# Turning the first unit's 47-point result on chip instead of through DRAM, and taking the token matrix's sums to GpSimd

## The chip, the cores and the metric

The kernel runs on one core of one Trainium2 chip. A core has five engines that each work through a queue of their own, in order: TensorE (PE in the profile; matrix products, with PEld for its weight loads), VectorE (DVE), ScalarE (ACT), GpSimd (POOL) and SyncE (SP, which here only issues DMAs). They meet at semaphores. SBUF is the on-chip memory that all of them read, PSUM is where the products land; DRAM is reached by DMA. The metric is the device time of one execution in microseconds (us), smaller is better. The kernel before takes 2456.34 us, the median of three runs (2453.95 to 2456.38).

## The reference

The input x is 8 batches of 3008 tokens with 256 channels. A Fourier stage comes first, then a token and channel mixer on its result:

```
X  = rfft(x, axis=1)                                # over 3008 tokens
Yr = Xr @ w_r - Xi @ w_i + b_r ;  Yi = Xr @ w_i + Xi @ w_r + b_i
Yr, Yi = soft_threshold(Yr, 0.01), soft_threshold(Yi, 0.01)
y  = irfft(Yr + 1j*Yi, n=3008, axis=1)              # batch, 3008, 256
h  = relu(y^T @ w_tok1) @ w_tok2                    # w_tok1 3008 x 256, w_tok2 256 x 3008
u  = y + h^T
out = u + relu(u @ w_ch1) @ w_ch2                   # 256 x 1536, 1536 x 256
```

x, w_r, w_i, b_r and b_i are float32; the four mixer weights (here `wt1`, `wt2`, `moe_w_ch1`, `moe_w_ch2`) are float64.

## The kernel before, in words

**The transform.** 3008 is 47 times 64, so the Fourier transform is a 47-point transform followed by a 64-point one. The 47-point part works on sums and differences of mirrored rows. Its rows are read in 13 groups of 5 x 24 = 120 rows (`NG = 13`, `GS = 5`, `KH = 24`), each with two halves `x[:, 0]` and `x[:, 1]`; the sum feeds a cosine matrix, the difference a sine matrix (`f1`, 120 x 120 blocks). `dft47` (L258) drives the 13 groups: `load`, then `sum_diff` (L220), then `stage1` (L233), which does the products, copies PSUM to SBUF and stores the result to a DRAM tensor. It is read back with the 64 x 2 rows of one pair of frequencies on the partitions, because the 64-point transform (`forward`, L414) takes its products over these. There are 12 such pairs, `kp` = 0 to 11.

**The units.** The 8 batches are treated as units `[0], [1], [2,3], [4,5], [6,7]`. Unit 0 is computed in `begin` (L547) with plain float32 products; the later units use pairs of rounded products (`mm3`, L174) and are woven into the channel mixer of the unit before them.

**What `begin` does.** It does two things side by side. One is unit 0: `forward` (line L421 does its products, L423 the copy from PSUM, L424 the third plane `xf` as a sum of the other two), `mix` (L441 the products with w_r and w_i, L446 to L448 the reads of PSUM with the bias on DVE, L450 to L452 the soft threshold, whose result stays in the tiles `held`), `inverse` (L469) and `tokens` (L484). The other is the token matrix w_tok1: its 13 groups are loaded as float64 (`raw`), made float32 by `narrow` (L144 to L156: two ACT instructions and six DVE instructions a group), passed through the same 47-point products as x, stored to the DRAM tensor `a_w`, read back (`load_w`) and taken through the 64-point transform in `make_w` (L317). Since the transform of y against the token matrix is taken in the frequency domain, `tokens` needs both.

For the token matrix the kernel before forms no sums. It puts both halves into the products (L250 to L252):

```
PE.matmul(pt[:120, o:o + w], lhsT=f1[:, i], rhs=sd[:, 0], start=True, stop=False)
PE.matmul(pt[:120, o:o + w], lhsT=f1[:, 2 * i], rhs=sd[:, 1], start=False, stop=True)
```

which is four products a group, where a sum and a difference would need two.

**The loop over steps.** After unit 0's 47-point part, `begin` runs steps n = 0 to 18. Step n takes the next two groups of the token matrix (until the 13 are done), `forward(n)`, `mix(n-1)`, `inverse(n-3)`, and from step 7 on `tokens` and `make_w`. Three groups of the token matrix are done ahead of step 0, so the groups end in step 4. The loads of unit 0's result from DRAM (`load_a`, L411) run three steps ahead. The float64 pieces of w_ch1 are narrowed and split in steps 8 to 13, those of w_ch2 and the first of w_tok2 after that. Then `channel` begins, the mixer over 49 chunks of at most 512 columns. It runs to the end of the kernel, with the later units' transforms woven in.

**What sets the order.** The order on each engine is a list that is fixed when the program is built; a scheduling layer makes it from the program's order and the tiles' buffers, so it is not exactly the source's order. Each engine takes its list in order and waits at the head for what the head needs. All products share four PSUM banks in rotation (`bank`, L129): a bank is written again only after ACT or DVE has read it. All loads, and unit 0's and the token matrix's stores, are on SP's queue, in order.

## Time and profile before

| what | value |
|---|---|
| runs | 2453.95, 2456.34, 2456.38 us |
| the profiled execution's own time | 2458.71 us |
| its span | 2456.7 us |
| PE busy | 2423.6 us (99%) |
| DVE, ACT, POOL busy | 1107.5 (45%), 873.3 (36%), 305.1 (12%) us |
| HBM read and written | 162.68 and 87.43 MB |

The profile's rows give a start and a length in us, the engine, the line of the code, the operation, the tile written and the tiles read, their sizes and how many instructions are merged. A float32 product appears as two records. In brackets stands the engine's idle time ahead of the row and what ended it. A matmul's recorded length contains some 0.16 us of pipeline, so the pace of TensorE is read from start to start. Rows of the "stretches" view give, for a stretch of time, the length, each engine's busy time with the number of records, the clock granted to TensorE (1.00 is full), the busy share of the DMA engines and GB/s.

### The profile page before, as it was taken

Reading aid. Unit: us, or ns where it says so; the run is one execution under the profiler, and the core shown is the slowest. Engines: PE = TensorE matmul, PEld = TensorE weight load, DVE = VectorE, ACT = ScalarE, POOL = GpSimd, SP = SyncE. Lnnn points to the kernel's source line nnn. Section 1 sums busy time; section 2 is a strip of 40 time slices with the busy share of each in tenths; the row PEclk is TensorE's granted clock in tenths of the full one; section 3 lists DMA queues with packets and bytes.
Section 4 is the critical chain, followed back from the end, with each engine's and each line's share of the span. In section 5 each row is a group of like instructions: output and inputs, shape, how many; then the busy total and the mean of one; then the engine's idle time right before and its main releaser. Section 6 shows DMA issues by size and latency. Waiting matters only on the chain.

```text
span 2456.7 us, 31566 instructions
## 1 busy us (share of the span) xinstructions
PE 2423.6 (99%) x12748; PEld 2108.6 (86%) x12748; DVE 1107.5 (45%) x1773; ACT 873.3 (36%) x1583; POOL 305.1 (12%) x259
## 2 busy tenths in 40 slices
PE   6999999999999999999999999999999999999999
PEld 5878999988888888888888898888888888888887
DVE  6975665454544444434344354434334333232332
ACT  4764444443334343333333343333333222222222
POOL 0000222222222111111111111111111000000000
PEclk8999999999999999999999999999999999999999
DMA  9775334552233462222222263222321112112110
GB/s 269 238 244 152 95 112 141 156 174 90 84 98 111 114 179 84 65 72 88 89 76 69 94 176 105 80 87 80 101 66 38 63 56 63 49 58 80 37 55 18
DMA packets 148946, 252.15 MB, mean 103 GB/s; under 512 B 11009, under 2 KB 101089, under 8 KB 148801
## 3 DMA queue, kind: packets, MB, share of 16 engines
q1 hardware_dynamic: 122289, 199.80, 27.2%
q10 hardware_dynamic: 26512, 50.34, 6.5%
q8 instruction: 100, 1.64, 0.3%
q14 instruction: 45, 0.37, 0.0%
HBM read 162.68 MB, written 87.43 MB: 102 GB/s over the span
## 4 chain that ended last, share of the span: by engine, by line
PE 93%; DMA 4%; DVE 1%; ACT 1%; SPq 0%; issue 0%; POOL 0%; DVEq 0%; ACTq 0%
PE ph L175 10%; PE ph L176 10%; PE po L175 10%; PE po L177 10%; PE po L176 10%; PE ph L177 10%; PE pu L708 4%; PE px L421 3%; PE pm L177 2%; PE pm L175 2%; PE pm L176 2%; PE pu L175 2%; PE pu L176 2%; PE pu L177 2%; PE gp L175 2%; PE gp L177 2%
## 5 line engine op out<-in xcount | busy, mean ns | idle before, releaser
L747 DVE SCALAR_TENSOR_TENSOR hlo<-ph,hh 128x512 fp32r<-128x512 f32 (+4 forms) x588 | 391.6, 667 | 646.0 <-ACT hh L746 643.0
L746 ACT ACTIVATE hh<-ph 128x512 fp32r<-128x512 f32 (+4 forms) x588 | 340.5, 580 | 815.8 <-PE ph L177 812.9
L175 PE MATMUL ph<-uh,w 128*128 128x512 f32 (+4 forms) x1176 | 456.0, 388 | 0.4 <-DVE hlo L747 0.3
L176 PE MATMUL ph<-ul,w 128*128 128x512 f32 (+4 forms) x1176 | 449.6, 382 | 0.3 <-DVE ul L717 0.3
L177 PE MATMUL ph<-uh,w 128*128 128x512 f32 (+4 forms) x1176 | 448.8, 382 | 0.0
L175 PE MATMUL po<-hh,w2h 128*128 128x512 f32 (+4 forms) x1176 | 448.7, 382 | 0.0
L176 PE MATMUL po<-hlo,w2h 128*128 128x512 f32 (+4 forms) x1176 | 448.1, 381 | 0.0
L177 PE MATMUL po<-hh,w2l 128*128 128x512 f32 (+4 forms) x1176 | 448.0, 381 | 0.0
L177 PEld LDWEIGHTS ph<-uh,w 128*128 128x128 f32 x1176 | 221.1, 188 | 39.4
L175 PEld LDWEIGHTS po<-hh,w2h 128*128 128x128 f32 x1176 | 221.1, 188 | 38.7
L176 PEld LDWEIGHTS po<-hlo,w2h 128*128 128x128 f32 x1176 | 221.0, 188 | 38.7 <-DVE hlo L747 0.2
L177 PEld LDWEIGHTS po<-hh,w2l 128*128 128x128 f32 x1176 | 220.9, 188 | 38.4
L175 PEld LDWEIGHTS ph<-uh,w 128*128 128x128 f32 x1176 | 221.5, 188 | 35.8 <-DVE hlo L747 1.4
L176 PEld LDWEIGHTS ph<-ul,w 128*128 128x128 f32 x1176 | 221.6, 188 | 34.6 <-DVE ul L717 0.7
L137 DVE TENSOR_TENSOR xtl<-xf,xth 128x768 fp32r<-128x768 f32 x84 | 80.5, 958 | 193.7 <-ACT xth L134 193.5
L715 ACT COPY uf<-pu 128x470 f32<-128x470 f32 (+23 forms) x188 | 62.6, 375 | 233.0 <-PE pu L708 233.0
L175 PE MATMUL pm<-wmh,xth 128*128 128x256 f32 x504 | 144.5, 287 | 0.1
L137 POOL TENSOR_TENSOR yl<-z,yh 128x512 fp32r<-128x512 f32 x72 | 92.7, 1288 | 413.2 <-ACT yh L134 413.2
L177 PE MATMUL pm<-wmh,xtl 128*128 128x256 f32 x504 | 142.5, 283 | 0.4 <-DVE xtl L137 0.3
L176 PE MATMUL pm<-wml,xth 128*128 128x256 f32 x504 | 142.4, 283 | 0.0
L708 PEld LDWEIGHTS pu<-g,b 96*128 96x128 f32 x1024 | 130.8, 191 | 3.4
L424 POOL TENSOR_TENSOR xf<-xf 128x256 f32<-128x256 f32 x84 | 69.7, 830 | 499.8 <-ACT xf L423 499.4
(124 smaller groups left out, 3213.5 us busy)
## 6 DMA issues: line engine op xcount, KB each, us to landing
wt<-wt_d SPq DMA_DIRECT2D x28, 940.0 KB, 5.5
x<-in_x SPq DMA_DIRECT2D x39, 480.0 KB, 4.3
a<-a_d SPq DMA_DIRECT2D x36, 512.0 KB, 3.9
b_d<-bt ACTq DMA_DIRECT2D x36, 512.0 KB, 3.3
out<-o SPq DMA_DIRECT2D x34, 512.0 KB, 2.8
a_d<-a ACTq DMA_DIRECT2D x36, 480.0 KB, 3.3
wt<-wt_d SPq DMA_DIRECT2D x21, 752.0 KB, 5.1
b<-b_d SPq DMA_DIRECT2D x32, 480.0 KB, 6.2
```

The source lines that it names most:

```text
L137: lo_eng.tensor_tensor(out=lo, in0=src, in1=hi.bitcast(F32), op=ALU.subtract)
L175: PE.matmul(out, lhsT=wh, rhs=xh, start=start, stop=False)
L176: PE.matmul(out, lhsT=wh, rhs=xl, start=False, stop=False)
L177: PE.matmul(out, lhsT=wl, rhs=xh, start=False, stop=stop)
L421: PE.matmul(pt[:, o:o + 128], lhsT=x, rhs=f2cols(2 * kp + ab), start=True, stop=True)
L424: (V if plain else G).tensor_tensor(out=xf[:, 0], in0=xf[:, 1], in1=xf[:, 2], op=ALU.add)
L708: PE.matmul(pt[:, s * TOKS:(s + 1) * TOKS], lhsT=b2[:, s, cs], rhs=g2[:, 0 if s0 + s == 0 else 1], start=False, stop=s == k - 1)
L715: S.copy(out=ufs[m][:, ct, lo - at:hi - at], in_=pt[:, lo - c0:hi - c0])
L746: S.activation(out=hh, in_=pt, func=AF.Relu)
L747: V.scalar_tensor_tensor(out=hlo, in0=pt, scalar=0.0, in1=hh.bitcast(F32), op0=ALU.max, op1=ALU.subtract)
```

## The change

- Unit 0's 47-point result no longer goes to DRAM. The products are turned round: the x group is the stationary operand and `f1` the moving one, so that the 256 channels come out on the partitions (two halves of 128). ACT copies each group into a tile `z` that stays in SBUF (`stage1_turned`). For each pair `kp`, `turn` takes four 128 x 128 products of `z` with the identity, which puts the 64 x 2 rows on the partitions, and ACT copies the PSUM bank to `a2`. 13 stores and 12 loads of the DRAM tensor `a_0` are gone, and four copies of one element that held back the w_r, w_i and bias loads.
- `sum_diff` always forms the sum on GpSimd. The difference is formed on the engine `eng`: on VectorE for units 0 and 1 (as before), on GpSimd for the later units (on VectorE before) and on GpSimd for the token matrix, which had no sums before and now takes two products a group.
- For unit 0, the third plane `xf` and the last subtraction of the soft threshold (`held`) go from VectorE to GpSimd.
- The order of loads and of steps: all of unit 0's x first, then the identity, `f2`, w_r, w_i, the biases and five `raw` tiles (five buffers where there were four); the token matrix's groups start in step 0, two a step, and end in step 6; they are loaded three ahead; the splits of w_ch1 come in steps 11 to 15, since `z` lies in their place until then.

```
-            raw = pool.tile([rows, n, 2], U32, name="raw", bufs=4)
+            raw = pool.tile([rows, n, 2], U32, name="raw", bufs=5)
...
-    def sum_diff(x, w, eng, pool):
-        if pool is not None and w == DT and eng is None:
-            return x
-        sd = t4([120, 2, w], "sd")
-        eng.tensor_tensor(out=sd[:, 0], in0=x[:, 0], in1=x[:, 1], op=ALU.add)
-        V.tensor_tensor(out=sd[:, 1], in0=x[:, 0], in1=x[:, 1], op=ALU.subtract)
+    def sum_diff(x, g, w, eng, pool):
+        sd = t4([120, 2, w], "sd") if pool is None else wk.tile([120, 2, w], F32, tag=("xtl", "xf", "wt", "et")[g % 4], name="sd", bufs=2)
+        G.tensor_tensor(out=sd[:, 0], in0=x[:, 0], in1=x[:, 1], op=ALU.add)
+        eng.tensor_tensor(out=sd[:, 1], in0=x[:, 0], in1=x[:, 1], op=ALU.subtract)
         return sd
...
-                elif not adds:
+                else:
                     PE.matmul(pt[:120, o:o + w], lhsT=f1[:, i], rhs=sd[:, i], start=True, stop=True)
-                else:
-                    PE.matmul(pt[:120, o:o + w], lhsT=f1[:, i], rhs=sd[:, 0], start=True, stop=False)
-                    PE.matmul(pt[:120, o:o + w], lhsT=f1[:, 2 * i], rhs=sd[:, 1], start=False, stop=True)
...
+    def stage1_turned(sd, z, g):
+        n = GS if g < NG - 1 else N2 - GS * (NG - 1)
+        pt = bank("p1")
+        for t in range(2):
+            for i in range(2):
+                o = (2 * t + i) * GS * KH
+                PE.matmul(pt[:, o:o + GS * KH], lhsT=sd[:, i, t * 128:(t + 1) * 128], rhs=f1[:, i], start=True, stop=True)
+        S.copy(
+            out=z.rearrange("p k (q n) -> p q n k", q=4)[:, :, g * GS:g * GS + n],
+            in_=pt[:, :4 * GS * KH].rearrange("p (q n k) -> p q n k", q=4, n=GS)[:, :, :n],
+        )
...
-        return dft47(load, a_w, DT, 2, None, pool)
+        return dft47(load, a_w, DT, 3, G, pool)
...
+        def turn(kp):
+            pt = bank("pz")
+            for ab in range(2):
+                for t in range(2):
+                    PE.matmul(pt[:, ab * C + t * 128:ab * C + (t + 1) * 128], lhsT=wc["z"][:, 2 * kp + ab, t * 128:(t + 1) * 128], rhs=wc["eye"], start=True, stop=True)
+            a2 = ld([128, 2, nb, C], "a2")
+            S.copy(out=a2.rearrange("p k b c -> p (k b c)"), in_=pt)
             return a2
...
-            (V if plain else G).tensor_tensor(out=xf[:, 0], in0=xf[:, 1], in1=xf[:, 2], op=ALU.add)
+            G.tensor_tensor(out=xf[:, 0], in0=xf[:, 1], in1=xf[:, 2], op=ALU.add)
...
-                V.tensor_tensor(out=yh, in0=y, in1=cl, op=ALU.subtract)
+                G.tensor_tensor(out=yh, in0=y, in1=cl, op=ALU.subtract)
...
-            x = dft47(p.load_unit, p.a, p.w, NG, V, early)
+            wc["eye"] = early.tile([128, 128], F32, name="eye")
+            z = wc["z"] = const.tile([128, KH, 2 * 128], F32, tag="w1", name="z")
+            x = dft47(p.load_unit, z, p.w, NG, V, early, True)
             next(x)
+            DMA.dma_start(out=wc["eye"], in_=io["eye"])
             DMA.dma_start(out=f2, in_=io["f2"])
+            load_mix()
+            for _ in range(5):
+                load_raw1()
...
-            a2s = {0: p.load_a(0)}
-            prepare_mix()
-            a2s[1] = p.load_a(1)
-            for _ in range(3):
-                next(w1)
-            a2s[2] = p.load_a(2)
+            a2s = {0: p.turn(0), 1: p.turn(1)}
+            next(w1)
...
-                    if n + 3 < KP:
-                        a2s[n + 3] = p.load_a(n + 3)
+                    if n + 2 < KP:
+                        a2s[n + 2] = p.turn(n + 2)
...
+                if n == KP - 1:
+                    wc["w1"] = const.tile([128, 2, 2, DF], F32R, tag="w1", name="w1")
+                if 0 <= n - KP + 1 < 5:
+                    split_w1(*pieces[n - KP + 1], wide.pop(n - KP + 1))
```

How this moves the instructions shows at three places. The first is TensorE's list at step 1: the last product or two of the token matrix's group ahead of `forward(1)` (`px`), and what follows up to `mix(0)` (`pm`). Before:

```order
L251 MATMUL p_424<-wide,f_69 120x256
L252 MATMUL p_424<-wide,f_69 120x256
L421 MATMUL px<-f_71,a_275 128x128 x4
L441 MATMUL pm_441<-wf_262,xf 128x256 x2
L441 MATMUL pm_442<-wsum,xf 128x256 x4
L251 MATMUL p_466<-wide,f_69 120x256
```

In the change the same place, with both of the step's groups (`p_382`, `p_402`) and the turn (`pz`):

```order
L242 MATMUL p_382<-sd,f_69 120x256 x2
L242 MATMUL p_402<-sd,f_69 120x256 x2
L431 MATMUL px<-f_71,a_263 128x128 x4
L419 MATMUL pz<-eye,z 128x128 x4
L451 MATMUL pm_422<-wf_114,xf 128x256 x2
L451 MATMUL pm_423<-wsum,xf 128x256 x4
```

A group has two products where it had four, they read the sums `sd` and not `wide`, and four products with the identity stand between `forward` and `mix`.

The second is VectorE's list from one `mix` (the three instructions that read `pm`) to the next narrowing of groups. Before (`held` and `xf` are unit 0's; `wide_456` and `wide_473` are two groups of the token matrix):

```order
L446 TENSOR_TENSOR z_449<-pm1_441,bias_74 128x512
L150 TENSOR_SCALAR wide_456<-wide_456 120x512
L447 TENSOR_TENSOR z_449<-pm2_442,z_449 128x256
L448 TENSOR_TENSOR z_449<-pm2_442,z_449 128x256
L151 TENSOR_SCALAR wide_456<-raw_354 120x512
L151 TENSOR_SCALAR wide_473<-raw_373 120x512
L152 SCALAR_TENSOR_TENSOR wide_456<-wide_456 120x512
L150 TENSOR_SCALAR wide_473<-wide_473 120x512
L153 TENSOR_SCALAR wide_456<-wide_456 120x512
L152 SCALAR_TENSOR_TENSOR wide_473<-wide_473 120x512
L452 TENSOR_TENSOR held_343<-z_449 128x512
```

In the change (the narrowing's lines are one higher, and `mix(0)` now stands behind seven groups):

```order
L456 TENSOR_TENSOR z_430<-pm1_422,bias_74 128x512
L156 TENSOR_TENSOR wide_387<-wide_387 120x512
L457 TENSOR_TENSOR z_430<-pm2_423,z_430 128x256
L458 TENSOR_TENSOR z_430<-pm2_423,z_430 128x256
L151 TENSOR_SCALAR wide_437<-wide_437 120x512
L152 TENSOR_SCALAR wide_437<-raw_296 120x512
L151 TENSOR_SCALAR wide_457<-wide_457 120x512
L153 SCALAR_TENSOR_TENSOR wide_437<-wide_437 120x512
L152 TENSOR_SCALAR wide_457<-raw_321 120x512
L154 TENSOR_SCALAR wide_437<-wide_437 120x512
L153 SCALAR_TENSOR_TENSOR wide_457<-wide_457 120x512
L155 TENSOR_TENSOR wide_437<-raw_296,wide_437 120x512
```

`held` and `xf` are gone from VectorE's list; the narrowing and the three reads of PSUM are what is left.

The third is GpSimd's list. Before, its first work is unit 1's (`wt`, the split of a weight block, and later `xf`, `y`):

```order
L137 ISA
L137 TENSOR_TENSOR wt_2305<-aw_2080,wt_2305 128x512
L137 TENSOR_TENSOR wt_2415<-aw_2084,wt_2415 128x512
L424 TENSOR_TENSOR xf_2095<-xf_2095 128x256
L424 TENSOR_TENSOR xf_2109<-xf_2109 128x256
L137 TENSOR_TENSOR y_2137<-z_2158,y_2137 128x512
```

In the change, one step's worth of it (`wide_367` to `wide_437` are groups 5 to 7 of the token matrix):

```order
L222 TENSOR_TENSOR sd_398<-wide_367 120x256
L223 TENSOR_TENSOR sd_398<-wide_367 120x256
L222 TENSOR_TENSOR sd_448<-wide_387 120x256
L223 TENSOR_TENSOR sd_448<-wide_387 120x256
L434 TENSOR_TENSOR xf_480<-xf_480 128x256
L462 TENSOR_TENSOR held_304<-z_430 128x512
L222 TENSOR_TENSOR sd_466<-wide_437 120x256
L223 TENSOR_TENSOR sd_466<-wide_437 120x256
```

Each step has six instructions there, on an engine that had none in `begin` but the two for `wt` at its end.

More of the change, by code (lines that the diff above doesn't have):

```diff
@@ L110, in _constants @@
         "f1": f1.astype(f),
+        "eye": np.eye(128).astype(f),
         "f2": f2.astype(f),
@@ L209, in tile_kernel @@
     a_d = [dram.tile([128, KH, 512], F32, name=f"a_d{p}") for p in range(2)]
-    a_0 = dram.tile([128, KH, C], F32, name="a_0")
     b_d = [dram.tile([NSLOT, 96, 512], F32, name=f"b_d{p}") for p in range(2)]
@@ L231, in split_x, with stage1 @@
         return xh, xl
-    def stage1(sd, dst, g, w, pool, adds):
+    def stage1(sd, dst, g, w, pool):
         n = GS if g < NG - 1 else N2 - GS * (NG - 1)
-        if pool is None:
-            a = ev([120, 2, w], "a")
-        elif adds:
-            a = pool.tile([120, 2, w], F32, name="a", bufs=4)
-        else:
-            a = wk.tile([120, 2, w], F32, tag=("xtl", "xf", "wt", "et")[g % 4], name="a", bufs=2)
+        a = ev([120, 2, w], "a") if pool is None else pool.tile([120, 2, w], F32, name="a", bufs=4)
         each = 512 // w
@@ L247, in stage1, with dft47 @@
                     mm3(pt[:120, o:o + w], f1r[:, 0, i], f1r[:, 1, i], sd[0][:, i], sd[1][:, i], True, True)
-                elif not adds:
+                else:
                     PE.matmul(pt[:120, o:o + w], lhsT=f1[:, i], rhs=sd[:, i], start=True, stop=True)
-                else:
-                    PE.matmul(pt[:120, o:o + w], lhsT=f1[:, i], rhs=sd[:, 0], start=True, stop=False)
-                    PE.matmul(pt[:120, o:o + w], lhsT=f1[:, 2 * i], rhs=sd[:, 1], start=False, stop=True)
             S.copy(out=a[:, i0:i0 + each].rearrange("p i w -> p (i w)"), in_=pt[:120])
-        wc["a"] = a
         rows = dst.rearrange("(i n) k w -> (n k) i w", i=2)
         (DMA if pool else PUT).dma_start(out=rows[g * 120:g * 120 + n * KH, :, :w], in_=a[:n * KH])
-    def dft47(load, dst, w, ahead, eng, pool=None):
+    def stage1_turned(sd, z, g):
[9 more added lines that the diff above has]
+        )
+    def dft47(load, dst, w, ahead, eng, pool=None, turned=False):
         xs = [load(g) for g in range(ahead)]
@@ L272, in dft47 @@
         prepare(0)
-        if pool is None:
-            prepare(1)
-            divide(0)
+        prepare(1)
+        divide(0)
         for g in range(NG):
@@ L278, in dft47 @@
                 xs.append(load(g + ahead))
-            prepare(g + (1 if pool else 2))
+            prepare(g + 2)
             divide(g + 1)
-            stage1(sds.pop(g), dst, g, w, pool, eng is None)
+            if turned:
+                stage1_turned(sds.pop(g), dst, g)
+            else:
+                stage1(sds.pop(g), dst, g, w, pool)
             yield 0.7 * w / C
@@ L341, in split_e, with load_mix @@
         return et
-    def prepare_mix():
-        wf = const.tile([128, 2, 2, C], F32, tag="gl", name="wf2")
-        for i in range(2):
-            V.tensor_copy(out=wf[:1, i, 0, :1], in_=wc["a"][:1, 0, :1])
-            V.tensor_copy(out=bias[:1, i, :1], in_=wc["a"][:1, 0, :1])
+    def load_mix():
+        wf = wc["wf2"] = const.tile([128, 2, 2, C], F32, tag="gl", name="wf2")
         for i, name in enumerate(("w_r", "w_i")):
@@ L387, in parts @@
         w = nb * C
-        a, bd = a_0 if plain else a_d[u % 2], b_d[u % 2]
+        a, bd = a_d[u % 2], b_d[u % 2]
         def load_unit(g):
@@ L401, in load_unit @@
             DMA.dma_start(out=x, in_=src[:, :, bs[0] % 2:bs[0] % 2 + nb])
-            if plain and g in (5, 8, 11):
-                load_raw1()
             return x.rearrange("q i b c -> q i (b c)")
@@ L560, in ahead @@
             wide[i] = narrow_w1(*pieces[i], early if i < 5 else None)
-            if i:
-                split_w1(*pieces[i - 1], wide.pop(i - 1))
         with tc.tile_pool(name="early", bufs=1) as early:
```

10 lines of the change are left out of this document (6 added, 4 removed).

## The prediction, made before the result was known

> **What bounds the kernel now.** First the page's busy times, then the stretches of time, then TensorE's rows in order of time.
>
> ```profile
> PE 2423.6 (99%) x12748; PEld 2108.6 (86%) x12748; DVE 1107.5 (45%) x1773; ACT 873.3 (36%) x1583; POOL 305.1 (12%) x259
> ```
>
> ```profile
> 0.00:29.00 29.00, 16.60 (x52) 11.64 (x53) 15.51 (x40) 12.33 (x24) 0.20 (x4) 0.90 0.88 237
> ...
> 94.00:165.00 71.00, 66.08 (x358) 50.05 (x359) 54.97 (x113) 46.41 (x98) 2.70 (x2) 1.00 0.80 247
> ...
> 240.00:2457.00 2217.00, 2209.30 (x11670) 1932.93 (x11668) 928.82 (x1400) 735.87 (x1324) 301.93 (x253) 1.00 0.30 89
> ```
>
> From 240 us on PE is idle for 7.7 of 2217 us at full clock, and the change gives PE no more and no less to do there. So only the preparation counts: the time moves by as much as the first product of `channel` moves, at 165.26.
>
> ```profile
> 27.49 2.06 PE L249 MATMUL p<-sd,f 120*120 120x256 f32 x4 [2.72 <-ACT a L253]
> 29.34 1.06 PE L251 MATMUL p<-wide,f 120*120 120x256 f32 x2
> ...
> 33.61 0.60 PE L252 MATMUL p<-wide,f 120*120 120x256 f32 x2
> ...
> 48.33 1.06 PE L421 MATMUL px<-f,a 128*128 128x128 f32 x8
> ...
> 58.09 0.60 PE L251 MATMUL p<-wide,f 120*120 120x256 f32 x2
> ...
> 61.55 1.06 PE L421 MATMUL px<-f,a 128*128 128x128 f32 x8
> ...
> 69.03 1.06 PE L421 MATMUL px<-f,a 128*128 128x128 f32 x8
> ...
> 76.88 1.06 PE L421 MATMUL px<-f,a 128*128 128x128 f32 x8
> ...
> 81.23 1.06 PE L421 MATMUL px<-f,a 128*128 128x128 f32 x8
> 82.12 1.02 PE L441 MATMUL pm<-wf,xf 128*128 128x256 f32 x4
> ...
> 84.71 1.03 PE L469 MATMUL pi<-held,ef 128*128 128x256 f32 x4
> 85.58 1.05 PE L421 MATMUL px<-f,a 128*128 128x128 f32 x8
> ...
> 91.68 1.89 PE L441 MATMUL pm<-wsum,xf 128*128 128x256 f32 x8
> ...
> 95.38 1.09 PE L317 MATMUL pw<-aw,fk 128*64 128x256 f32 x8
> ```
>
> ```profile
> 165.26 0.38 PE L175 MATMUL ph<-uh,w 128*128 128x470 f32 x1
> ```
>
> By these starts PE needs 0.89 us for `forward` (four 128-column products, 0.22 each), 2.59 for `mix`, 0.87 for `inverse`, and 0.43 for one 256-column product (eight from 58.09 to 61.55). Steps with two groups of the token matrix take 7.5 and 7.9 us (61.55 to 69.03 to 76.88); without groups 4.4. VectorE tells why:
>
> ```profile
> 97.28 0.42 DVE L151 TENSOR_SCALAR wide<-raw 128x512 uint32<-128x512 uint32 x1
> 97.62 0.68 DVE L154 TENSOR_TENSOR wide<-raw,wide 128x512 f32<-128x512 f32 x1
> 98.22 0.68 DVE L152 SCALAR_TENSOR_TENSOR wide<-wide 128x512 uint32<-128x512 uint32 x1
> 98.82 0.68 DVE L155 TENSOR_TENSOR wide<-wide 128x512 f32<-128x512 f32 x1
> ```
>
> Back to back, a 512-wide instruction on two tensors occupies DVE for 0.60 us, one on a tensor and a scalar for 0.33. A group is three of each, 2.8; `mix` reads PSUM for 0.60 + 0.33 + 0.33 = 1.27; `held` 0.60, `xf` (256 wide) 0.33. Two groups and one of each make 7.8: **VectorE sets the pace** of these steps, not PE.
>
> **The change, part by part.** It takes 0.93 us a step from DVE and gives POOL six instructions a step. What these cost alone:
>
> ```profile
> 250.74 0.74 POOL L424 TENSOR_TENSOR xf<-xf 128x256 f32<-128x256 f32 x1 [0.64 <-ACT xf L423]
> ...
> 269.35 1.29 POOL L137 TENSOR_TENSOR y<-z,y 128x512 fp32r<-128x512 f32 x1 [4.13 <-ACT y L134]
> ```
>
> Four sums and differences and `xf` at 0.74, `held` at 1.29: 4.97 us a step, below DVE's remaining 6.87. Were the two independent, a step would be 7.0 (PE: 4 x 0.43 + 0.89 + 0.89 for the turn + 2.59 + 0.87). They are not:
>
> ```profile
> 156.35 0.65 DVE L154 TENSOR_TENSOR wide<-raw,wide 128x470 f32<-128x470 f32 x1
> 156.79 1.34 POOL L137 TENSOR_TENSOR wt<-aw,wt 128x512 fp32r<-128x512 f32 x1 [156.35 <-ACT wt L134]
> ...
> 157.04 1.60 DVE L155 TENSOR_TENSOR wide<-wide 128x470 f32<-128x470 f32 x1
> ...
> 161.00 1.36 POOL L137 TENSOR_TENSOR wt<-aw,wt 128x512 fp32r<-128x512 f32 x1 [2.87 <-DMA w_d<-wf]
> 162.10 0.53 DVE L151 TENSOR_SCALAR wide<-raw 128x470 uint32<-128x470 uint32 x1 [0.87 <-DMA raw<-in_wt]
> ```
>
> ```profile
> L225 DVE TENSOR_TENSOR sd<-x 120x512 f32<-120x512 f32 x39 | 41.2, 1056 | 3.5 <-POOL y L137 1.6 <-DMA x<-in_x 1.2 <-POOL yl L137 0.2
> L446 DVE TENSOR_TENSOR z<-pm,bias 128x512 f32<-128x512 f32 x96 | 65.5, 683 | 25.6 <-PE pm L177 25.5
> ```
>
> The 470-wide L155 began 0.25 us after a POOL instruction, took 1.60 us in place of 0.65, and ended 0.51 after POOL did. L225, which runs beside POOL's sum of the same x, has a mean of 1.06 us where such an instruction takes 0.68. L446, which reads PSUM, keeps 0.683 over 96 instructions. So a VectorE instruction that takes its tensors from SBUF stands still while POOL works, and all six of the narrowing do that; 0.13 us of its length (0.65 less 0.51) it saves behind the wait.
>
> **The step.** 6.87 + 4.97, less POOL's share beside the three PSUM reads (1.27 of 6.87, so 0.9), less six times 0.13: 10.2 us. POOL and DVE taking turns is the bound; the 11.2 us that PE saves on 26 products and the eight turns inside these steps both vanish under it.
>
> [...]
>
> **The beginning.** Unit 0's x, the constants and the first `raw` now go in that order.
>
> ```profile
> x<-in_x SPq DMA_DIRECT2D x26, 240.0 KB, 4.7
> raw<-in_wt SPq DMA_DIRECT2D x13, 480.0 KB, 7.8
> ...
> aw<-a_w SPq DMA_DIRECT2D x12, 256.0 KB, 3.7
> ...
> a_w<-a SPq DMA_DIRECT2D x12, 240.0 KB, 6.1
> ```
>
> 13 x 240 KB, 480 KB and 1.2 MB of constants (by their shapes) are 4.9 MB; at the 237 GB/s of the first stretch that is 20.7 us, so the first `raw` lands at 22.7. Its narrowing, entangled with the next two groups', takes 5.3 us; then two POOL instructions: first product at 29.5, against 29.34. Nothing is gained there. The turned first stage (52 products of 120 columns against 26 of 256, both 11 us), its 13 ACT copies and POOL's sums lie under x's landing, which ends by 17 (3.4 MB from 2 us on, at that rate); two turns lie in the wait for `raw`. What the removed stores cost was the place in SP's list:
>
> ```profile
> 19.82 10.75 SPq L256 DMA_DIRECT2D a<-a  x12
> ```
>
> Twelve of `a_0`'s stores held SP, in order, until 30.6, with the fourth `raw` behind them, and PE then had no group from 36.6 to 42.4. That gap goes, and so does the wait of step 0 for `a_0` (48.33); step 0 now follows the second group at about 31. ACT takes 12 more copies of 0.58 us, one a step, where it is busy for 46 of 71 us: hidden, and with that cover gone 7 us. The turn also takes one of the four PSUM banks in rotation, so that the next step's `forward` waits for DVE to read the `mix` before; that wait is PE's share of DVE's pace and not a term of its own.
>
> From 28.0 to `mix(0)` on DVE its list has 15.2 us of narrowing, and POOL has eleven 0.74 us instructions, each holding it for 0.61: 28.0 + 15.2 + 6.7 = 49.9. Three steps of 10.2 bring `mix(3)` to 80.5. The times before:
>
> ```profile
> 58.21 0.68 DVE L446 TENSOR_TENSOR z<-pm,bias 128x512 f32<-128x512 f32 x1
> ```
>
> ```profile
> 80.39 0.68 DVE L446 TENSOR_TENSOR z<-pm,bias 128x512 f32<-128x512 f32 x1
> ```
>
> The removed trip of `a_0` through DRAM gives a lead of 8 us at `mix(0)`; at `mix(3)` it is used up. Up to `mix(6)` DVE's list has four pieces of w_ch1 (11.2 us), three mixes' worth (3.8), and POOL 7.5 us, of which 5.4 hold it: 80.5 + 15.0 + 5.4 = 100.9. PE's products of `mix(6)` cannot end much earlier, since the banks of `mix(5)` are freed by the same list; before they ended at 93.4 (91.68 + 8 x 0.215). **So step 7 is 7.5 us late.** The token matrix's last group leaves PE at about 90; copy, store (6.1) and load (3.7) bring it back at 101.5, when `make_w` wants it: no stall, and none to spare.
>
> After that PE has two more turns on its path, 1.8 us. Of the 4.9 us that it idles from 94 to 165, waits for transfers, I count 1 as saved by being late (bounds 0 and 3). DVE has 36 us and POOL 14 left for 70. In the later units 39 differences go to POOL, under PE's work: 0, bound 3 either way. **Sum:** 7.5 + 1.8 - 1 = +8.3 us on a profiled execution of 2458.7, which lies 2.4 above the median; the median becomes 2456.3 + 8.3, rounded to 2465.
>
> **The rivals.** *POOL runs beside DVE.* Then steps take 7.0, the first stretch 15.2, `mix(3)` is done at 64.5, the last group at 72, and the stored matrix sets the end: back at 83, against `make_w` at 95.38: -12.4 + 1.8, 2446 us. For it: POOL's 4.97 fits into a step; against it the 1.60 row. 0.12.
>
> *Only the two-tensor instructions are held,* 3.6 of 6.87 us: POOL finds room beside the rest, a step is 8.7, `mix(0)` at 47.5, `mix(3)` at 73.6, `mix(6)`'s products end at 91.6: -1.8 + 1.8, 2456 us. For it: only one narrow tensor-scalar case shows a wait. 0.20.
>
> *TensorE's clock falls in the steps.* PE has 7.0 us of work in 10.2. After 2.7 idle us, at 27.49, its products came at 0.85 us instead of 0.43 (two from 29.34 take 1.06) up to 33.6. If each step's gap does that, 3 to 6 us at half speed cost 1.5 to 3 a step; while `mix` waits for PE and PE for banks (steps 4 to 7) this adds up: +6 to +12 on the forecast, 2474 us. Against it: the steps before had gaps and kept 1.00 from 60 us on. 0.13.
> [...]
>
> That the turn doesn't take the DRAM trip away is no rival: the loads are gone from SP's list.
>
> **How the numbers follow.** The forecast has 0.55. What a measurement of this kernel tells from no change is about 0.2%, 4.9 us. Slower: most of the forecast and the clock's case, 0.65. Same: most of the second rival and the forecast's low end, 0.20. Faster: the first rival and the second's low end, 0.15. The range goes from 2449, which takes in the second rival and leaves out most of the first, to 2475, which takes in most of the clock's case. The forecast's own is 2461 to 2470: a step of 9.7 to 10.7, three times, and the bounds of 3.
>
> **What would show it.** In the changed profile the narrowing's tensor-tensor instructions beside POOL average well over 0.68 us, L456's own stays at 0.68; `mix` rows on DVE lie near 50, 60, 70, 80 and `mix(6)` near 101; PE idles some 3 us a step up to step 7; the first `channel` product lies near 173. It is wrong if steps of two groups take under 9 us, if `make_w` waits for `a_w` by more than 2 us, or if PE's idle time after 240 us is more than 11 us.

## The result, and the profile after

| | runs | median (lowest to highest), us |
|---|---|---|
| before | 4 | 2455.87 (2453.95 to 2456.38) |
| changed | 4 | 2473.70 (2473.07 to 2473.98) |

The ratio is 1.0074, with a 95% interval of 1.0056 to 1.0091: the change makes the kernel **slower by about 18 us**, where +8.3 was forecast. Profile against profile it is 15.1 us (span 2471.8 against 2456.7); the kernel before was profiled in a run 2.8 us above its median.

The page's busy times, and the stretches of time of the changed kernel (busy us of each engine with records, granted clock, DMA share, GB/s):

```profile
PE 2429.4 (98%) x12844; PEld 2120.6 (86%) x12844; DVE 1077.3 (44%) x1680; ACT 882.1 (36%) x1595; POOL 433.8 (18%) x374
```

```profile
29.00:60.00 31.00, 19.78 (x96) 16.76 (x96) 23.64 (x43) 17.12 (x31) 21.20 (x16) 0.73 0.68 172
60.00:94.00 34.00, 29.41 (x135) 25.03 (x134) 31.95 (x53) 21.19 (x38) 20.81 (x20) 0.85 0.57 167
...
240.00:2472.00 2232.00, 2224.30 (x11759) 1947.02 (x11757) 900.90 (x1366) 739.16 (x1331) 341.79 (x292) 1.00 0.30 89
```

From 240 us on TensorE is idle for 7.7 us, as before. Nearly all that was lost was lost ahead of `channel`. The clock granted to TensorE is what differs most: 0.73 and 0.85 in the second and third stretch, where the kernel before had 0.82 and 1.00:

```profile
29.00:60.00 31.00, 23.96 (x95) 18.96 (x94) 25.72 (x58) 16.20 (x28) 0.00 (x0) 0.82 1.00 297
60.00:94.00 34.00, 33.26 (x176) 28.87 (x175) 31.78 (x68) 25.31 (x45) 0.00 (x0) 1.00 0.81 256
```

The marks on the way, `mix` on VectorE and then TensorE's `forward` of step 8 and first `channel` product:

```profile
55.39 0.68 DVE L456 TENSOR_TENSOR z<-pm,bias 128x512 f32<-128x512 f32 x1
...
84.21 0.68 DVE L456 TENSOR_TENSOR z<-pm,bias 128x512 f32<-128x512 f32 x1
...
105.25 0.68 DVE L456 TENSOR_TENSOR z<-pm,bias 128x512 f32<-128x512 f32 x1
```

```profile
106.30 1.16 PE L431 MATMUL px<-f,a 128*128 128x128 f32 x8
...
179.87 0.38 PE L176 MATMUL ph<-uh,w 128*128 128x470 f32 x1
```

These are `mix(0)`, `mix(3)` and `mix(6)`: a step takes (84.21 - 55.39) / 3 = 9.6 us. VectorE's rows leave no gap in these steps: it is busy, its waiting for GpSimd included, for all of the 40.7 us from 48.29 to 89.00. Step 7 is over, and step 8's `forward` begins, 9.9 us later than before (96.40); the first `channel` product comes 14.6 us later (165.26).

The groups of VectorE instructions from 29 to 95 us (count, busy us, mean ns) show the turns between the two engines. Alone, the first takes 0.68 us and the second 0.42:

```profile
L155 DVE TENSOR_TENSOR wide<-raw,wide 120x512 f32<-120x512 f32 x12 | 10.9, 909 | 0.0
...
L154 DVE TENSOR_SCALAR wide<-wide 120x512 uint32<-120x512 uint32 x12 | 7.7, 642 | 0.0
...
L456 DVE TENSOR_TENSOR z<-pm,bias 128x512 f32<-128x512 f32 x5 | 3.4, 680 | 2.0 <-POOL held L462 2.0
```

What nobody had counted on is one instruction of GpSimd, the sum of the token matrix's second group, and TensorE's wait for it:

```profile
35.25 8.00 POOL L222 TENSOR_TENSOR sd<-wide 120x256 f32<-120x256 f32 x1 [3.46 <-DVE wide L156]
43.21 0.72 POOL L223 TENSOR_TENSOR sd<-wide 120x256 f32<-120x256 f32 x1
```

```profile
43.30 2.06 PE L242 MATMUL p<-sd,f 120*120 120x256 f32 x4 [10.53 <-POOL sd L222]
```

```profile
42.25 0.42 DVE L152 TENSOR_SCALAR wide<-raw 120x512 uint32<-120x512 uint32 x1
48.29 0.49 DVE L151 TENSOR_SCALAR wide<-wide 120x512 f32<-120x512 f32 x1 [5.62 <-ACT wide L149]
```

It took 8.00 us instead of 0.72. VectorE worked without a pause from 32.27 to 42.67, with none of its instructions longer than alone, and GpSimd's sum ended at 43.25, 0.58 us after VectorE had run out of input. So the two took no turns there at all. TensorE stood for 10.5 us, and its next two products took 1.86 us (to 45.16, where the next row starts) instead of 0.86. ScalarE stood behind it, and VectorE's pause of 5.62 us is the end of this chain: the ScalarE instruction that it waited for (L149) stands in ScalarE's list behind the copy of these products.

```profile
45.40 0.58 ACT L243 COPY a<-p 120x512 f32<-120x512 f32 x1 [8.76 <-PE p L242]
```

### The profile page after: what moved, and what is told of

Same layout as the page of the kernel before. It is cut to its first block, busy times and chain, and to the rows that moved or that the text cites. A ratio compares the mean times of both kernels' runs of the same rounds, so it can differ in the third digit from the quotient of the medians.

```text
span 2471.8 us, 31798 instructions
## 1 busy us (share of the span) xinstructions
PE 2429.4 (98%) x12844; PEld 2120.6 (86%) x12844; DVE 1077.3 (44%) x1680; ACT 882.1 (36%) x1595; POOL 433.8 (18%) x374
## 4 chain that ended last, share of the span: by engine, by line
PE 93%; DMA 2%; DVE 2%; ACT 1%; POOL 1%; SPq 1%; issue 1%; DVEq 0%; ACTq 0%
PE ph L176 10%; PE po L177 10%; PE po L178 10%; PE po L176 10%; PE ph L177 10%; PE ph L178 10%; PE pu L720 4%; PE px L431 3%; PE pm L178 2%; PE pm L176 2%; PE pm L177 2%; PE pu L176 2%; PE pu L177 2%; PE pu L178 2%; PE gp L176 2%; PE gp L178 2%
## 5 line engine op out<-in xcount | busy, mean ns | idle before, releaser
L434 POOL TENSOR_TENSOR xf<-xf 128x256 f32<-128x256 f32 x96 | 80.5, 838 | 454.5 <-ACT xf L433 450.7
```

The lines of the kernel that those rows point to most:

```text
L434: G.tensor_tensor(out=xf[:, 0], in0=xf[:, 1], in1=xf[:, 2], op=ALU.add)
```

## The experiments

They stand in the order of the argument. Theory A is the prediction's: the turns of VectorE and GpSimd set the pace. B blames the turn of z on TensorE. D came out of the 8.00 us row: VectorE's unbroken run keeps GpSimd out. C, E and F are told where they come up. Every program gets its lists from the scheduling layer anew, so an edit can also change the order of instructions that it does not touch.

**1. The turn alone.** GpSimd gets nothing that it did not have before.

```
-        return dft47(load, a_w, DT, 3, G, pool)
+        return dft47(load, a_w, DT, 3, None, pool)
...
-            G.tensor_tensor(out=xf[:, 0], in0=xf[:, 1], in1=xf[:, 2], op=ALU.add)
+            (V if plain else G).tensor_tensor(out=xf[:, 0], in0=xf[:, 1], in1=xf[:, 2], op=ALU.add)
...
-                G.tensor_tensor(out=yh, in0=y, in1=cl, op=ALU.subtract)
+                V.tensor_tensor(out=yh, in0=y, in1=cl, op=ALU.subtract)
```

With `None` the groups go through the four products of the kernel before, and the sums of x go back to its engines.

> The change without anything on GpSimd that was not there before: the token matrix takes four products a group again and forms no sums, xf, held and the sums and differences of the x groups are on the engines of before. The turn, the new order of loads and of steps stay. Theory A (VectorE and GpSimd taking turns at SBUF makes the steps 9.6 us long and keeps TensorE waiting for the second group's sum for 10.5 us): both go; a step is 8.7 us by TensorE's own work (eight products of 0.43, 0.89 forward, 0.89 turn, 2.59 mix, 0.87 inverse), no wait over 3 us between 31 and 95 us, step 8's forward near 94 us, and with two turns (1.8) after it the time is within 3 us of before: 2453 to 2459. Theory B (the turn is what costs: its PSUM bank, its products and TensorE's halved clock after gaps): the time stays at 2468 or more.

Measured: 2465.85 us, ratio 1.0042 (1.0025 to 1.0059). Neither theory's number. The stretches from 30 to 95 us and step 8:

```profile
30.00:60.00 30.00, 28.06 (x151) 24.14 (x152) 27.40 (x60) 19.31 (x35) 0.00 (x0) 0.94 0.80 213
60.00:95.00 35.00, 33.11 (x182) 28.61 (x181) 31.37 (x68) 23.10 (x41) 0.00 (x0) 1.00 0.57 170
```

```profile
97.55 1.16 PE L436 MATMUL px<-f,a 128*128 128x128 f32 x8
```

TensorE works nearly through (its idle times from 35.6 to 97.6 us add up to 3.2), at full clock from 60 us on, and yet comes to step 8 1.15 us later than before. The kernel before had lost 6.8 us in two waits for groups in this stretch (5.6 of them ahead of 42.37); the turns of the steps up to there cost TensorE eight times 0.89 us. **The turn exchanges idle time for work of about the same length.** Behind that come two more turns and a wait of 3.4 us for `a_w`, so that the turn by itself is a loss. By the two profiles it is 6.8 us, 4.0 of them ahead of the first `channel` product (169.25 against 165.26); the rest lies behind it and was not followed.

**2. GpSimd's part alone**, in the kernel before: sums and differences of the token matrix, `xf`, `held`, the sums of x and the later units' differences as in the change; unit 0's trip through DRAM and all orders as before.

```
-        return dft47(load, a_w, DT, 2, None, pool)
+        return dft47(load, a_w, DT, 2, G, pool)
```

(with `sum_diff`, `xf` and `held` as in the change, and two products a group)

> The kernel before, with unit 0's trip through DRAM and the order of loads and steps as they were, and with GpSimd's new work: sums and differences of the token matrix (two products a group), xf and held of unit 0, the sums of x and the later units' differences. Theory A: the steps with two groups go from 7.5 and 7.9 us to 9.6 or more, three of them, and the gap before step 0 takes up a part: +2 to +8, 2458 to 2464. Theory B: TensorE has 11 us less to do and nothing is lost: 2448 to 2456.

Measured: 2483.40 us, ratio 1.0112 (1.0097 to 1.0127), far over both. TensorE's rows at the beginning:

```profile
36.69 5.04 PE L248 MATMUL p<-sd,f 120*120 120x256 f32 x12 [7.74 <-POOL sd L223]
51.92 3.77 PE L248 MATMUL p<-sd,f 120*120 120x256 f32 x8 [10.18 <-POOL sd L223]
```

The second wait holds a sum that GpSimd needed 6.12 us for. In this order the token matrix has no lead, and both waits fall on TensorE. The run is also not the change's second part alone: its sums lie in tiles that unit 0's results use until their stores are through, which the change does not have. The two parts do not add up (10 and 27 us apart, 18 together): with the turn's order of loads, GpSimd's part costs 8.

**3. The first three groups' sums on VectorE.**

```
+        add = G
+        if pool is not None and eng is G and g < 3:
+            add = eng = V
-        G.tensor_tensor(out=sd[:, 0], in0=x[:, 0], in1=x[:, 1], op=ALU.add)
+        add.tensor_tensor(out=sd[:, 0], in0=x[:, 0], in1=x[:, 1], op=ALU.add)
```

> The change, with the sums and differences of the token matrix's first three groups on VectorE instead of GpSimd (six instructions of about 0.34 us more in VectorE's list). Theory A (GpSimd's sum of the second group took 8.00 us because VectorE's unbroken run of instructions kept it out of SBUF): TensorE's wait of 10.5 us ahead of the second group falls to 1 to 4 us, the first mix row on VectorE comes at 47 to 50 instead of 55.4, steps stay at 9.6 us: 2464 to 2468. Theory C (the 8.00 us are GpSimd's own or a wait for something else, and the rest of the program sets the start): less than 3 us are gained: 2471 or more.

Measured: 2475.99 us, ratio 1.0084 (1.0069 to 1.0099); nothing gained. The row of 8.00 us is gone, but the long rows came back elsewhere: `xf` took 5.04 us at 42.56 and 5.71 at 74.12, a sum 5.73 at 67.22. By its number theory C (the 8.00 us are GpSimd's own) would stand; the rows contradict it, since each of these, too, ended 0.6 to 0.7 us after VectorE had stopped or had begun to read PSUM.

**4. All sums of the token matrix on VectorE**: as in 3, without `and g < 3`.

> The change, with all sums and differences of the token matrix on VectorE; xf and held stay on GpSimd. VectorE has 6.87 + 4 x 0.34 = 8.2 us a step, GpSimd 2.03, of which 1.8 hold VectorE when they take turns. Theory A: no starved sum at the start (8 us gained), steps of 9.4 us: 2460 to 2466. Theory B: 2470 or more, since the turn and TensorE's list are as in the change.

Measured: 2471.36 us, ratio 1.0060 (1.0045 to 1.0075), above theory A's range and inside B's. GpSimd has two instructions a step left, and one of them is kept out at once, with TensorE behind it:

```profile
52.16 2.07 PE L454 MATMUL pm<-wf,xf 128*128 128x256 f32 x4 [5.71 <-POOL xf L437]
```

That `xf` was kept out from 43.99 for 8.11 us. Fewer instructions on GpSimd helped little here (2471.36 against 2473.70 us), with TensorE waiting for one that was kept out.

**5. When GpSimd gets in, measured by itself.** Two kernels of their own, with runs of VectorE instructions and single GpSimd sums. In the first the order of GpSimd's independent sums came out differently from what was meant: twenty of them were drawn together into one row, so that its stages s4, s5, s7 and s8 do not measure what their names say.

> A kernel of its own that computes nothing of the reference: it measures when a GpSimd sum (256 columns, SBUF, 0.72 us alone) gets through beside runs of VectorE instructions (512 columns). In s1 the run is 21 sums from SBUF, in s2 21 tensor-scalar instructions, in s3 21 sums of PSUM and SBUF, in s4 and s5 there are six GpSimd sums (s5 mixes the two kinds), in s6 the run has one PSUM instruction at place 9; GpSimd's first sum is ready after the third instruction. In s7 and s8 GpSimd has begun a row of six and VectorE comes in. In s9 each VectorE instruction reads what ScalarE copied just before it. Theory D (a run of SBUF instructions without a pause keeps GpSimd out for as long as it lasts): in s1, s2 and s5 GpSimd ends about 0.58 us after the run's last instruction, a first sum of some 11, 6 and 8 us; in s3 it takes 0.72; in s6 it gets in at the PSUM instruction, after 3.6 us. Theory E (the two take turns, each waiting for at most one instruction of the other, as the prediction had it): no GpSimd sum is over 1.4 us in any stage.

Measured: in the row of sums the two engines alternated strictly (1.21 us for a VectorE instruction, 1.17 for a sum, so one of each in 1.13 us), as theory E has it. One sum that became ready inside a long run was kept out for **26.2 us**, through 48 VectorE instructions, until one read PSUM. Both theories were right somewhere, and what decides between them was the question of the second kernel.

> A kernel of its own that computes nothing of the reference. VectorE begins each of 17 stages after a real pause (it waits for GpSimd's last sum), works through a run without pauses on 512 columns in SBUF, and one GpSimd sum (0.72 us alone) becomes ready inside the run. Stages 1 to 6: two-tensor instructions (0.60 us each), 2, 3, 4, 5, 6 and 8 of them ahead of GpSimd's sum, 12 behind. Stages 7 to 12: tensor-scalar instructions (0.335), 4, 6, 7, 8, 9 and 12 ahead, 20 behind. Stages 13 to 15: 8 ahead, and after four more an instruction that reads PSUM, one that reads a single element of PSUM, one that reads a single element of SBUF. Stages 16 and 17: 5 ahead, a PSUM instruction (512 columns, one element), 2 more, then the sum. Theory D in the form that the traces suggest (turns are taken while VectorE's run is younger than some 2.9 us; from then on GpSimd waits until the run pauses or reads PSUM): a sum of about 1.1 us in stages 1 to 3 or 4, over 5 us in stages 5 and 6; 0.8 to 1.1 us in stages 7 to 9 or 10, over 4 us in 11 and 12; in 13 about 3 us. If the number of instructions decides and not the time, stages 1 to 5 and 7 to 9 part at the same count, six or seven. Theory E (turns always): no sum over 1.4 us.

Measured, the rows of GpSimd's sum in stages 4 and 5, 7 and 8, 13 and 15 (start, length):

```profile
39.80 1.04 POOL L165 TENSOR_TENSOR p<-g,b 128x256 f32<-128x256 f32 x1 [10.38 <-DVE g L142]
51.82 7.66 POOL L165 TENSOR_TENSOR p<-g,b 128x256 f32<-128x256 f32 x1 [10.98 <-DVE g L142]
...
74.76 0.77 POOL L165 TENSOR_TENSOR p<-g,b 128x256 f32<-128x256 f32 x1 [2.07 <-DVE g L145]
84.66 7.14 POOL L165 TENSOR_TENSOR p<-g,b 128x256 f32<-128x256 f32 x1 [9.13 <-DVE g L145]
...
140.89 2.85 POOL L165 TENSOR_TENSOR p<-g,b 128x256 f32<-128x256 f32 x1 [5.54 <-DVE g L142]
...
167.40 2.84 POOL L165 TENSOR_TENSOR p<-g,b 128x256 f32<-128x256 f32 x1 [10.38 <-DVE g L142]
```

It is the number of instructions and not the time: a sum that came 3.70 us into a run of 0.60 us instructions got the next turn (stage 4), one that came 2.71 us into a run of 0.335 us instructions did not (stage 8). With the stage's first instruction counted, a sum that came during the seventh instruction or earlier took its turn (1.04 us in stage 4); one that came during the eighth or later waited until the run ended (stages 5, 6, 8 to 12, 16 and 17: 7.14 to 8.27 us, 0.58 us after the run's end), until an instruction read PSUM (stage 13: 2.85 us), or until one of a single element came, even in SBUF (stages 14 and 15: 2.85 and 2.84 us, in at that instruction). My 2.9 us were wrong, the effect was not. The place of the limit is sure to one instruction only: in the changed kernel VectorE's run began at 32.27 after a pause of 1.74 us, the sum of 35.25 came during the run's seventh instruction, and it was kept out. In the second kernel VectorE pauses for 0.03 us behind each stage's first instruction; if the run is counted from there, the last to get in is the sixth, and the two agree.

What the runs show goes beyond turns: a sum that came late in a run was kept out from one VectorE instruction to the next (8.00 us in the change, 26.2 us in the first of the two kernels). Why a number of instructions decides it, no run shows.

**6. All of it on VectorE.** Sums and differences of the token matrix, `xf` and `held` (the edits of 1 for `xf` and `held`, and of 4).

> The change, with the token matrix's sums and differences, xf and held all on VectorE, so that GpSimd has nothing to do in the steps. VectorE has 7.8 + 4 x 0.34 = 9.2 us a step, TensorE 7.0. Theory D: no instruction is kept out, no TensorE wait over 3 us between 40 and 95 us, steps of 9.2 us by VectorE alone: 2460 to 2468, below the change's 2473.7. If VectorE's own work were all that counts, GpSimd's part in the change costs nothing: 2472 or more.

Measured: 2471.66 us (2465.85 to 2473.38), ratio 1.0054 (1.0036 to 1.0072): between the two cases, and hardly better than with GpSimd. There are no GpSimd instructions in the steps, and still a step takes 11.3 us (`mix(1)` and `mix(3)`, two steps apart):

```profile
64.23 0.68 DVE L459 TENSOR_TENSOR z<-pm,bias 128x512 f32<-128x512 f32 x1
...
86.74 0.68 DVE L459 TENSOR_TENSOR z<-pm,bias 128x512 f32<-128x512 f32 x1
```

```profile
60.00:95.00 35.00, 28.08 (x132) 24.41 (x133) 29.43 (x69) 18.68 (x33) 0.00 (x0) 0.85 0.54 159
```

VectorE is busy for 29.4 of 35 us, so its own work is not the bound; TensorE is busy for 28.1, at a clock of 0.85. That opened theory F, that the slower TensorE makes the steps long (experiment 9). VectorE's pauses in these two steps, and what ScalarE waited for ahead of the instruction (L464) that ends them:

```profile
70.63 0.69 DVE L465 TENSOR_TENSOR held<-z 128x512 f32<-128x512 f32 x1 [2.44 <-ACT z L464]
...
81.45 0.69 DVE L465 TENSOR_TENSOR held<-z 128x512 f32<-128x512 f32 x1 [1.56 <-ACT z L464]
```

```profile
67.67 0.58 ACT L424 COPY a<-pz 128x512 f32<-128x512 f32 x1 [1.12 <-PE pz L422]
...
80.12 0.68 ACT L149 ACTIVATE wide<-raw 128x512 f32<-128x512 f32 x1 [1.35 <-DMA raw<-in_moe_w_ch]
```

In the first step ScalarE's soft threshold (L463, L464) stands in its list behind the copy of a turn that TensorE did at half pace (1.71 us, from 65.72 to 67.43, instead of 0.89). In the second L464 stands behind the narrowing of a piece of w_ch1 that had not landed, which is not the clock's doing.

**7. Only `xf` and `held` back on VectorE** (the two edits of 1).

> The change, with xf and held back on VectorE; the token matrix's sums and differences stay on GpSimd. VectorE 7.8 us a step, GpSimd 2.96. Theory D: the sum of the second group is still kept out for some 8 us and TensorE waits about 10 us for it, the waits for xf and held are gone: 2466 to 2473. By turns alone (the prediction's step): 9.4 us a step instead of 10.2, 2468.

Measured: 2475.13 us, ratio 1.0075 (1.0059 to 1.0091). The long row is there as theory D says (7.07 us at 44.81, TensorE waiting 7.3), the waits for `xf` and `held` are gone, and the time is the change's.

**8. The run broken.** The change with two copies of one element in each narrowing.

```
         V.scalar_tensor_tensor(out=u0, in0=u0, scalar=3, in1=u1, op0=ALU.logical_shift_left, op1=ALU.bitwise_or)
+        V.tensor_copy(out=t1[:1, :1], in_=t0[:1, :1])
...
         V.tensor_tensor(out=t0, in0=t0, in1=t1, op=ALU.add)
+        V.tensor_copy(out=t1[:1, :1], in_=t0[:1, :1])
```

> The change, with one edit: in the narrowing of every float64 tile VectorE gets two copies of a single element in SBUF (0.06 us each), after its third and after its last instruction, so that its runs hold a short instruction at least every six. Theory D (an unbroken run keeps GpSimd out): no GpSimd instruction of the steps takes over 3 us, TensorE's wait of 10.5 us ahead of the second group falls to 3 or 4, the wait of 2.3 us for held at 148.7 goes: 2461 to 2468. If being kept out is only a symptom, because VectorE's and GpSimd's work together or the chain through TensorE and ScalarE sets the pace: the long GpSimd rows go, the time stays at 2470 or more.

Measured: 2474.87 us, ratio 1.0073 (1.0058 to 1.0088), the change's own time. The copies do what they should: the longest GpSimd row of all the steps is 2.56 us, TensorE's longest wait 4.3. And the stretches:

```profile
30.00:60.00 30.00, 21.80 (x100) 16.82 (x100) 30.00 (x59) 19.69 (x35) 16.44 (x18) 0.80 0.71 184
60.00:95.00 35.00, 27.60 (x130) 23.36 (x131) 34.97 (x69) 20.16 (x35) 18.07 (x18) 0.85 0.54 158
```

VectorE, its waiting for GpSimd included, is occupied for 64.97 of 65 us. **Being kept out was not what set the time.** With it gone the turns alone fill the whole stretch, and `mix(6)`, which stands behind 17 narrowings in both kernels, comes at 104.6 instead of 105.25. The 28 copies take some 1.8 us of that themselves (0.06 to 0.07 each), so up to 2.5 us can be put down to the long rows.

**9. The products twice.** The kernel of 6, with more work for TensorE:

```
+                    for _ in range(2 if eng is G else 1):
-                    PE.matmul(pt[:120, o:o + w], lhsT=f1[:, i], rhs=sd[:, i], start=True, stop=True)
+                        PE.matmul(pt[:120, o:o + w], lhsT=f1[:, i], rhs=sd[:, i], start=True, stop=True)
```

> The kernel with all sums, xf and held on VectorE (GpSimd idle), with one edit: each product of the token matrix's groups is done twice into the same place, so that TensorE has as many products as with no sums (8.7 us a step instead of 7.0). Nothing else changes. If TensorE's halved clock after its idle times makes those steps 11 us where VectorE has 9.2 (Theory F): the granted clock from 60 to 95 us rises from 0.85 to over 0.95, steps fall to 9.2 to 9.8 us, 2462 to 2468. If the clock is not what counts: steps of 11 us and more, 2471 to 2482.

Measured: 2466.12 us (2463.22 to 2468.55), ratio 1.0037 (1.0023 to 1.0051). `mix` in the same two steps, and the stretch:

```profile
63.10 0.69 DVE L460 TENSOR_TENSOR z<-pm,bias 128x512 f32<-128x512 f32 x1
...
81.42 0.70 DVE L460 TENSOR_TENSOR z<-pm,bias 128x512 f32<-128x512 f32 x1
```

```profile
60.00:95.00 35.00, 34.72 (x193) 30.31 (x192) 35.00 (x81) 21.76 (x38) 0.00 (x0) 1.00 0.63 188
```

With 26 useless products a step is 9.2 us, to the tenth VectorE's own work, the clock is 1.00, and the first `channel` product comes 7.1 us earlier (170.94 against 178.03). These are the signs that theory F named. But the products are not all that differs: the lists of TensorE, ScalarE and VectorE came out in another order than in 6. TensorE does a step's groups ahead of `forward` and not in between, and ScalarE's soft threshold (L464 and L465 here) stands ahead of the turn's copy and of the next narrowing, so that VectorE's two pauses ahead of `held` could have gone by the order too. The clock and the order are not separated, and **theory F is supported, not shown**. In the times the gain is 5.5 us, and the two ratios' intervals overlap, so its size is not settled; the kernel of 6 itself spread over 7.5 us.

**10. The turn in one pass.** The kernel of 1 with z and the identity rounded to fp32r; what that costs in the output's precision was not measured:

```
-            wc["eye"] = early.tile([128, 128], F32, name="eye")
-            z = wc["z"] = const.tile([128, KH, 2 * 128], F32, tag="w1", name="z")
+            eye = early.tile([128, 128], F32, name="eye")
+            wc["eye"] = early.tile([128, 128], F32R, name="eyer")
+            z = wc["z"] = const.tile([128, KH, 2 * 128], F32R, tag="w1", name="z")
...
-            DMA.dma_start(out=wc["eye"], in_=io["eye"])
+            DMA.dma_start(out=eye, in_=io["eye"])
+            S.copy(out=wc["eye"], in_=eye)
```

> The change without GpSimd's part (as in the first experiment), with one edit: z and the identity are rounded to fp32r, so that the four products of a turn take 0.06 us each in place of 0.22; the output has a lower precision for that. TensorE has 8.0 us a step instead of 8.7, VectorE 7.8. If the turn costs TensorE time (Theory A's reading of the first experiment: no idle time from 35 to 97 us): 5 to 8 us less than the 2465.9 there, 2457 to 2461. If its bank, its copy on ScalarE or the order of the loads cost: 2463 or more.

Measured: 2462.08 us over ten runs, ratio 1.0024 (1.0015 to 1.0034), between the two cases. A turn's four products took 0.48 us (96.82 to 97.30) in place of 0.89, where 0.24 was expected. Step 8 comes at 95.91 instead of 97.55: TensorE's idle times from 35.5 to 96 us grew from 3.2 to 4.7, of which 4.0 (all 3.2 in experiment 1) end with ScalarE's copy of a group's products. So the turn's time on TensorE is a part of its loss, though the intervals of the two ratios overlap. What remains against the kernel before, 4.9 us by the medians and 1.8 by the two profiles, lies behind step 8, which comes 0.5 us earlier than before: TensorE waits 2.9 us there for `gh`, which stands behind the conversion of a late piece of w_ch2 in ScalarE's list. It is not settled by a run of its own.

**11. Before, with unit 0's stores on ScalarE's queue.**

```
-        (DMA if pool else PUT).dma_start(out=rows[g * 120:g * 120 + n * KH, :, :w], in_=a[:n * KH])
+        (DMA if adds else PUT).dma_start(out=rows[g * 120:g * 120 + n * KH, :, :w], in_=a[:n * KH])
```

> The kernel before with one edit: unit 0's thirteen stores go out on ScalarE's queue instead of SP's, so that SP does not wait at them with the fourth raw load behind (until 30.6 us). If that place in SP's list was what the trip through DRAM cost, the TensorE gap of 5.6 us ahead of 42.4 goes and the time falls by 3 to 6 us: 2450 to 2453. If the gap has another cause, or VectorE only has the same list to work off, 2454 to 2458.

Measured: 2465.70 us, ratio 1.0038 (1.0024 to 1.0052): slower, which neither case had. The stores held ScalarE in their turn, its first `narrow` instruction came at 31.8 us (19.8 before), and the loads of x landed later. It moved too much to say anything on SP's list; that the stores' place there cost the gap at 42 us stays open.

## Why the prediction was right, and where it was not

**Direction and mechanism: right.** The instructions of both kinds are lengthened beside GpSimd (0.909 against 0.68 us on two tensors; 0.642 against 0.42 on a tensor and a scalar, for which the profile before had only L151's 0.53 us), the one that reads PSUM is not (0.680), TensorE has no more idle time after 240 us, and VectorE, with its waits for GpSimd, is busy without a gap from 48.29 to 89.00 us, as it is in experiment 8. A step was forecast at 10.2 us and took 9.6: 6.87 of VectorE's own and 2.7 of waiting for six GpSimd instructions. `make_w` waited for `a_w` by 0.9 us at most. Two of the signs did not come: the first `channel` product lies at 179.87 and not near 173, and TensorE does not idle for 3 us a step. Its waits from 45 to 95 us add up to 5.2 us in five steps; the rest of its slack went into products at half pace (the forward, turn and mix from 67.90 to 74.81 took 6.9 us, where 4.4 were counted). Two sums of the working are slightly off, 4.97 (4.99) and 101.5 (100.4 by its terms); the forecast does not hang on them.

**The size: half.** Step by step, each against the kernel before:

| | forecast | measured |
|---|---|---|
| end of step 7 | +7.5 | +9.9 |
| two more turns | +1.8 | +1.8 |
| idle time behind it | -1 | +1.8 |
| the rest of that stretch | 0 | +1.1 |
| after the first `channel` product | 0 | +0.5 |
| sum, profile to profile | +8.3 | +15.1 |

The third line is TensorE's idle time from step 8's `forward` to `channel`: 4.7 us before, 6.4 after; the fourth is a remainder, what is left of that stretch's growth (73.6 us against 68.9).

- *Step 7* is late by the beginning. VectorE began on the first `raw` at 23.97 instead of 22.7 and ended its narrowing at 29.93 instead of 28.0, with splits of the `mix` weights in between that the sum had left out, so all marks were 1.9 us late from the start. `mix(0)` came 5.5 us late: the working had VectorE busy throughout, and it stood idle for 1.74 and 5.62 us, the second at the end of the chain behind the 8.00 us row. The steps, shorter than forecast, made up 1.8 of that by `mix(3)`. That the time from the narrowing to `mix(6)` comes out near the forecast (72.9 us forecast, 75.3 in the change) is partly luck: it holds 9.4 us in which VectorE was idle, and GpSimd held it for less than was counted.
- *The term of -1* is the one that failed, with its bounds (0 to 3 us absorbed). Being late did not save waits, it made others. TensorE's waits from 94 to 180 us in the changed kernel (total, times, longest):

```profile
PE pi L479 <- POOL held L462: 2.3, 1, 2.3
PE pu L176 <- ACT gh L503: 2.0, 1, 2.0
PE pw L321 <- ACT w2h L135: 1.0, 1, 1.0
PE pw L321 <- DMA aw<-a_w: 0.9, 1, 0.9
```

  The first is a GpSimd instruction that took 4.16 us instead of 1.29 in a stretch that I had called free ("DVE has 36 us and POOL 14 left for 70"); the second is the late w_ch2 load, whose issue stood behind a load of `a_w` in SP's list. After the wait for `gh` the clock was halved: products of 470 columns came every 0.39 us, until 175.6, where they took 0.21 before.
- *That each waits for at most one instruction of the other* was assumed, by counting 0.61 us a GpSimd instruction, and is wrong from the seventh or eighth instruction of a run on. It explains the 10.5 us wait and the 2.3 us one. By experiment 8 it cost little up to `mix(6)` (0.7 us, or 2.5 with the copies taken off), because the steps were full anyway.

**The rivals.** That GpSimd runs beside VectorE, and that only two-tensor instructions are held, fall with the rows of 0.909 and 0.642 us. *TensorE's clock* gave 2474 us, the time measured, and its sign is in the profile (0.73 and 0.85). The stretches at half speed that it counts on are in the profile before (granted clock 0.64 and 0.51 from 16 to 20 us, 0.50 from 28 to 32), and the changed kernel has them behind its waits too (0.58, 0.50, 0.50 and 0.71 from 66 to 74 us, 0.70 and 0.50 from 86 to 90, in stretches of 2 us). Yet in the change's own steps VectorE has no gap that a faster TensorE could close. Where TensorE's pace can have cost time is ahead of them, where VectorE waited at the end of the chain (from 43.30 to 46.86 two products and a `forward` took 3.56 us instead of 1.75, by which I estimate up to 1.8 us), and behind step 8, within the 1.1 us of the fourth line. So this rival came to the right number, but for the most part not by its own mechanism: that is luck. Whether the products done twice would help the change itself was not tried.

**What I had not seen is that three limits lie close together**: TensorE's own work with the turn (8.7 us a step with four products, an estimate added up from the starts in the profile before), VectorE's with the sums (9.2), and the turns with GpSimd (9.6). That is why taking one away never gained more than a few us, and why the 11.2 us of products saved on TensorE (26 of 0.43) were worth nothing. Without GpSimd and with the products saved the steps took 11.3 us; whether TensorE's clock or the order of the lists made them that long is open.

## What to carry to other kernels

Before work is moved from a busy engine to a free one, look for what the two share: here a 256-column sum on GpSimd held VectorE for 0.53 us (1.13 less 0.60, experiment 5), more than the 0.33 us in which VectorE does such a sum itself, and TensorE had a new engine to wait for. Work that is taken from TensorE in a stretch where it does not set the pace gains nothing there (here 11.2 us of products); look at the granted clock afterwards, which fell here from 1.00 to 0.85. When an experiment's edit looks small, compare the engines' lists before believing that nothing else changed. And when an experiment removes the most visible wait and gains nothing, the next limit is right behind it: look at which engine is now busy all the time.

## What the runs showed of the hardware

- GpSimd and VectorE alternated in SBUF for 20 GpSimd sums in a row (1.13 us for one 512-column VectorE instruction and one 256-column sum). But a sum that became ready late in a run of VectorE was kept out to the run's end: from the eighth instruction on in the second kernel of experiment 5, at the seventh in the change; 26.2 us at the longest. A VectorE instruction that reads PSUM, or one of a single element (0.06 us), let it in.
- An instruction that reads PSUM or has a single element *ahead* of GpSimd's sum did not make the run young again (stages 16 and 17: 7.66 and 8.27 us). In experiment 3 the sum of 5.73 us began at the end of the second of two instructions that read PSUM, and was kept out all the same.
- With 26 repeated products the granted clock from 60 to 95 us was 1.00 instead of 0.85 and the steps took 9.2 us instead of 11.3; the order of the lists changed with it, so the clock alone is not shown to be the cause.
